# Where experts with few tokens are computed: 64-token steps of their own, or f32 pieces between the layers of a 256-token block

## The chip, the cores and the metric

The kernel runs on one core of one Trainium2 chip. The metric is the device time of one execution in microseconds (us), the median over three runs. Engines are called by their names or by the profile's short forms: TensorE (PE, its weight loads PEld), VectorE (DVE), ScalarE (ACT), GpSimd (POOL), and SyncE (SP), which here only issues DMAs. A q behind a short form (PEldq) means the engine's queue: branches, waits, loads of registers.

## The reference, cut to what matters

Three stages follow one another. Attention with a window gives `x` with 2304 tokens of 512 values. A mixture of 8 experts with one expert per token follows, then a dense block of two layers.

```python
e_idx = np.argmax(logits, axis=1)            # logits = x @ w_gate + modality_bias[modality_id]
...
for e in range(E):                           # E = 8
    mask = e_idx == e
    if not mask.any():
        continue
    h = np.maximum(x[mask] @ w1[e], 0.0)     # w1[e] 512 x 1024
    out[mask] = gate_w[mask, None] * (h @ w2[e])   # w2[e] 1024 x 512
...
h = x @ w_in                                 # 512 x 2048, then a quadratic relu
return (g @ w_out).astype(np.float32)        # 2048 x 512
```

How many tokens an expert gets depends on the data. With the inputs that `setup_inputs` draws (seed 0), the reference sends 19, 1735, 3, 0, 540, 6, 0 and 1 tokens to experts 0 to 7.

## The kernel before, in words

Everything large is computed in fp32r with the operands split into a hi and a lo half: three matmuls (hi x hi, lo x hi, hi x lo) stand for one f32 product. An expert's weights are 8 tiles of 128 x 1024 values (512 KB each, `raw`), four of `w1` and four of `w2`. `Weights.split` makes `whi` (a cast on ScalarE) and `wlo` (a subtraction on VectorE or GpSimd) of each.

The expert stage is a list of steps laid out at build time, up to 17, of which the counts decide at run time which do what. Small tables of the counts are computed on VectorE (`Route.late_counts`, `Route.registers`), written to the tile `ri` and loaded into registers of the engines (`Moe.values`, line 506). The expert with the most tokens among the first 512 goes first (here expert 1), and two half blocks of it are gathered while attention still runs. After that, experts come in cyclic order. Each expert's tokens fill blocks of 256 columns. A last block of at most 64 tokens runs in a narrow form, and a remainder of at most 64 beyond a full block makes that block 320 wide. With these inputs the steps are: 1 to 6 for expert 1, 7 narrow for expert 2, 8 and 9 (320 wide) for expert 4, 10 to 12 narrow for experts 5, 7 and 0. Steps 13 to 16 are skipped.

`Moe.step(s)` writes a step's work out in a fixed order: `layer1`, then gathers of later tokens on GpSimd and the first four weight splits for the next step (`resplit`), then loads of weights on SP, then `layer2`, the scaling of the gathered tokens on VectorE, the other four splits and loads. Every engine runs its own part in that order. `layer1` and `layer2` have three arms each (narrow, 256, 320), chosen by a register (lines 729, 747, 754, 767); every engine jumps over the arms that it doesn't take.

- `l1_wide(fb)`, eight times: 12 matmuls of 256 columns (line 587), a relu on ScalarE, the lo half of `h` on VectorE. Four PSUM banks (`A`) take turns.
- `l2_wide(d)`, four times: 24 matmuls, one copy to `xy` on ScalarE. Two banks (`B`).
- the narrow arms swap the operands: 64 tokens with hi and lo are the stationary operand (128 columns), the weights move (512 columns, lines 612 and 613). A matmul with `fold` (lines 619 and 764) adds the halves and transposes back.
- `tx`: eight transposes that bring the next step's tokens into `xh` and `xl`.

Between these runs `Convert`: it turns `w_in` and `w_out` (int64 words) into f32, in 32 parts of six VectorE operations (lines 813 to 825; the first can be ScalarE's), and stores them to DRAM (`wsc`). `CV_STEPS` says how many parts each step does in its first and second half: 20 in steps 2 to 5 and 12 in steps 6 to 8. Its loads and stores stand in SP's queue among the loads of expert weights. `Blocks` reads `wsc` back and splits it for the dense part, which goes over six groups of 384 tokens and writes each token to its place by an indirect DMA. `Route.positions` computes these places.

Of the kernel before, what the change touches and what calls it, by code (L numbers as in the profile page):

```python
# [23 lines left out]
HP = H // 2  # L24
# [26 lines left out]
YW = N + 192  # L51
# [3 lines left out]
LOADS = (0, 2, 1, 3, 4, 6, 5, 7)  # L55
R_M, R_CN, R_NE, R_C, R_D, R_O, R_N = range(7)
# [40 lines left out]
def body(ctx, tc, qT, kT, vW, mod, w_gate, m_bias, w1, w2, w_in, w_out, cst, msk, out):  # L97
# [9 lines left out]
    oh = keep.tile([128, NT + 1, E], BF16, name="oh")  # L107
# [4 lines left out]
    tri16 = const.tile([128, 128], BF16, name="tri16")  # L112
    one16 = const.tile([128, 128], BF16, name="one16")

    m2 = None
    with ExitStack() as st:
        banks = Banks(tc, st)
# [12 lines left out]
        cv.loads()  # L130
        late = ExitStack()
        for s in range(2, NS):
            moe.step(s, cv, m2, late=late)
            if s == CV_LAST:
                cv.close()
                m2 = Blocks(tc, ctx, wsc)
                m2.first()
        late.close()
    dense(tc, xy, m2, pid, out)


# [63 lines left out]
class Route:  # L205
    def __init__(self, tc, cs, oh, tri16, one16, banks, moe, pid):
# [25 lines left out]
        self.sm = p.tile([1, 8, 18], F32, name="rt_sm")  # L232
        self.sa = p.tile([1, 17, E], F32, name="rt_sa")
# [50 lines left out]
    def pick(self):  # L284
# [12 lines left out]
        V.tensor_scalar(self.sm[:, 0, 0:1], self.r8[0:1], -1.0, 8.0, op0=ALU.mult, op1=ALU.add)  # L297
        V.tensor_copy(self.moe.ri[:, R_M, 0:1], self.sm[:, 0, 0:1])
# [13 lines left out]
    def early_counts(self):  # L312
# [26 lines left out]
        V.tensor_scalar(self.pr[:, :, E], self.nAm, -1.0, None, op0=ALU.mult)  # L339

# [17 lines left out]
    def late_counts(self):  # L358
# [8 lines left out]
        V.tensor_scalar(self.k8, self.nM, 0.0, 256.0, op0=ALU.is_gt, op1=ALU.mult)  # L367
# [9 lines left out]
        hi, HI = self.tmp[:, :, E], self.HI  # L377
        V.tensor_tensor(HI, self.look[:, 0, :], hi, op=ALU.add)
        V.tensor_tensor(self.look[:, 1, :], hi, self.look[:, 1, :], op=ALU.is_ge)
        V.tensor_scalar(self.look[:, 0, :], HI, -0.5, 3968.0, op0=ALU.mult, op1=ALU.add)  # L380
        V.tensor_tensor(self.look[:, 0, :], self.look[:, 0, :], self.look[:, 1, :], op=ALU.mult)
        V.tensor_tensor(HI, HI, self.look[:, 0, :], op=ALU.add)
# [7 lines left out]
    def lookup(self, table, dst):  # L390
# [3 lines left out]
        nc.vector.tensor_reduce(dst, self.tmp, axis=AX.X, op=ALU.add)  # L394
# [4 lines left out]

    def rest_columns(self):  # L400
        self.columns(0, NT, self.HI, 16, 32)
# [5 lines left out]
    def registers(self):  # L407
        nc, cs, ri = self.tc.nc, self.cs, self.moe.ri
        P0 = slice(0, 1)
        b3, b4 = [1, 16, E], [1, 17, E]  # L410
        ta = cs[P0, C_TAU:C_TAU + 32:2]
        et, ex, cf, off, rem, u, mk, db = (self.sm[:, i, 0:17] for i in range(8))
        a, a4 = self.sa[:, 0:16], self.sa
        b8 = [128, E, E]
        V = nc.vector
        nb, ts, kk, q1 = self.nM[P0], self.tab[P0, 0, :], self.t8[P0], self.k8[P0]
        nAm, key = self.nAm[P0], self.key[P0]
        V.tensor_tensor(ts, ts, nAm, op=ALU.add)
        V.scalar_tensor_tensor(kk, nb, 0.0, key, op0=ALU.is_gt, op1=ALU.mult)
        V.tensor_tensor(a, ts.unsqueeze(1).to_broadcast(b3), ta.unsqueeze(2).to_broadcast(b3), op=ALU.is_le)  # L420
        V.tensor_tensor(a, a, kk.unsqueeze(1).to_broadcast(b3), op=ALU.mult)
        V.memset(et[:, 0:1], 0.0)
        V.tensor_reduce(et[:, 1:17], a, axis=AX.X, op=ALU.max)
        V.memset(cf[:, 0:1], 1.0)
        V.tensor_tensor(cf[:, 1:17], et[:, 1:17], et[:, 0:16], op=ALU.not_equal)
        V.tensor_copy(ri[:, R_C, 0:17], cf)
        V.tensor_tensor(a, key.unsqueeze(1).to_broadcast(b3), et[:, 1:17].unsqueeze(2).to_broadcast(b3), op=ALU.is_equal)
        V.tensor_tensor(q1, nb, ts, op=ALU.add)
        V.tensor_tensor(self.v[P0, 0:16], a, q1.unsqueeze(1).to_broadcast(b3), op=ALU.mult)
        V.tensor_reduce(rem[:, 1:17], self.v[P0, 0:16], axis=AX.X, op=ALU.add)  # L430
        V.tensor_tensor(rem[:, 1:17], rem[:, 1:17], ta, op=ALU.subtract)
        V.tensor_scalar(u[:, 1:17], rem[:, 1:17], 256.0, None, op0=ALU.is_gt)
        V.scalar_tensor_tensor(u[:, 1:17], rem[:, 1:17], 320.0, u[:, 1:17], op0=ALU.is_le, op1=ALU.mult)
        V.scalar_tensor_tensor(ri[:, R_D, 1:17], rem[:, 1:17], 64.0, u[:, 1:17], op0=ALU.is_gt, op1=ALU.add)
# [12 lines left out]
        V.tensor_tensor(self.pr[:, :, 0:E], self.nS.unsqueeze(1).to_broadcast(b8), self.tri, op=ALU.mult)
        V.tensor_reduce(self.s1, self.pr[:, :, 0:E], axis=AX.X, op=ALU.add)
        V.tensor_reduce(db[:, 0:1], self.n1[P0], axis=AX.X, op=ALU.add)
        V.tensor_scalar(ri[:, R_N, 0:1], db[:, 0:1], 1.0 / 256, None, op0=ALU.mult)  # L450
        V.tensor_scalar(u[:, 1:17], ta, db[:, 0:1], float(N), op0=ALU.is_ge, op1=ALU.mult)
        V.tensor_tensor(q1, self.s1[P0], nAm, op=ALU.add)
        V.tensor_tensor(q1, q1, ts, op=ALU.subtract)
        V.tensor_tensor(a, key.unsqueeze(1).to_broadcast(b3), et[:, 1:17].unsqueeze(2).to_broadcast(b3), op=ALU.is_equal)
        V.tensor_tensor(a, a, q1.unsqueeze(1).to_broadcast(b3), op=ALU.mult)
        V.tensor_reduce(off[:, 1:17], a, axis=AX.X, op=ALU.add)
        V.tensor_tensor(off[:, 1:17], off[:, 1:17], ta, op=ALU.add)
        V.tensor_tensor(off[:, 1:17], off[:, 1:17], u[:, 1:17], op=ALU.max)
# [17 lines left out]
class Moe:  # L476
    def __init__(self, tc, st, cs, xy, x_dram, w, banks):
# [4 lines left out]
        self.x = one.tile([128, HP, 5, 2, 64], F32R, name="x")  # L482
        self.xh, self.xl = self.x[:, :, :, 0, :], self.x[:, :, :, 1, :]
        self.h, self.hh, self.hl = [], [], []
        self.hidden(one)
        self.ids = one.tile([128, 2 * NS + 16], U32, name="ids")
        self.ri = one.tile([1, 7, NS], I32, name="ri")
# [3 lines left out]
    def hidden(self, pool):  # L491
        t = pool.tile([128, 4, 5, 2, 64], F32R, name=f"h{len(self.h)}")
        self.h.append(t)
        self.hh.append(t[:, :, :, 0, :])
        self.hl.append(t[:, :, :, 1, :])

    def rest(self, st):
        one = st.enter_context(self.tc.tile_pool(name="m_two", bufs=1))
        self.hidden(one)
        self.hs = one.tile([128, 2, 512], F32, name="hs")  # L500
        self.xg3 = one.tile([64, XW], F32, name="xg3")
        self.tc.nc.gpsimd.memset(self.xg3, 0.0)
# [6 lines left out]
    def expert(self, v):  # L509
        return self.tc.nc.s_assert_within(v, 0, E - 1, skip_runtime_bounds_check_because=BOUNDED)  # L510

    def load_first(self):
        return self.expert(self.values(R_M, R_M, 0, 1, [ENG.SP])[0])

    def load_sp(self, a, b):
        v = self.values(R_CN, R_NE, a, b, [ENG.SP])
        for i in range(b - a):
            r = self.regs.setdefault(a + i, {})
            r["cn"], r["ne"] = v[i], self.expert(v[b - a + i])

    def load_mode(self, a, b):
        c = self.values(R_C, R_C, a, b, [ENG.Activation, ENG.DVE, ENG.Pool])
        d = self.values(R_D, R_D, a, b, [ENG.PE, ENG.Activation, ENG.DVE, ENG.Pool])
        dp = self.values(R_D, R_D, a, b, [ENG.Pool])
        dv = self.values(R_D, R_D, a, b, [ENG.DVE])
# [130 lines left out]
    def load_w(self, s, a, b):  # L656
        if s >= NS:
            return
# [639 lines left out]
```

## Time and profile before

| | |
|---|---|
| median of 3 runs | 875.83 us (875.2 to 876.02) |
| profiled execution | 875.21 us, span 873.4 us |
| mean granted TensorE clock | 0.965 |
| PE busy | 796.6 us (91%) |
| PEld busy | 727.0 us (83%) |
| DVE busy | 523.3 us (60%) |
| ACT busy | 302.5 us (35%) |
| POOL busy | 150.5 us (17%) |
| loads of expert weights | 48 of 512 KB |

Times are counted from the span's start. Attention takes the time until about 130 us, the expert steps that until 454 us, dense the rest. [...] An engine's idle time is put down to what ended it; "issue" means that nothing in the profile was waited for. A plain f32 matmul leaves two records in the trace, an fp32r matmul or a transpose one.

### The profile page before, as it was taken

What the parts mean: (1) busy time and instruction counts of PE and PEld (TensorE: products, weight loads), DVE (VectorE), ACT (ScalarE), POOL (GpSimd) and SP (SyncE); (2) the same over time, 40 slices, a digit from 0 to 9 for tenths busy, and PEclk for the clock granted to TensorE, in tenths of its full rate; (3) what the DMA queues carried; (4) which work ended last, traced back from release to release, by engine and by line L of the source; (5) the groups of instructions that cost most, each with busy time, mean ns of one, the idle gap of its engine ahead of it and who ended that gap; (6) DMA issues with size and microseconds to landing.
All of it is one profiled execution on the core that took longest, in us unless ns stands there. A gap on an engine that the chain in (4) does not pass through costs nothing. (4 is left out here: it accounts for less than half of the span.)

```text
span 873.4 us, 15586 instructions
## 1 busy us (share of the span) xinstructions
PE 796.6 (91%) x5735; PEld 727.0 (83%) x5737; DVE 523.3 (60%) x1110; ACT 302.5 (35%) x775; POOL 150.5 (17%) x118
## 2 busy tenths in 40 slices
PE   8999698999998966699568999999999999999996
PEld 4887598999998956698467999999999999999995
DVE  4798967557767899547945764434434434444441
ACT  3665552222222343234333443223223223223221
POOL 2335632000000343025620001000000000000001
PEclk9999999999999988899697999999999999999999
DMA  7788633635656588526612420000000000000000
GB/s 188 225 249 266 200 104 87 226 131 189 207 155 223 195 277 285 164 76 198 207 32 76 144 73 25 13 1 24 13 1 25 13 2 13 24 1 13 25 2 36
DMA packets 54243, 96.23 MB, mean 110 GB/s; under 512 B 7104, under 2 KB 24512, under 8 KB 54112
## 3 DMA queue, kind: packets, MB, share of 16 engines
q1 hardware_dynamic: 49920, 80.71, 28.9%
q0 software_dynamic: 4048, 13.51, 5.2%
q8 instruction: 78, 1.28, 0.6%
q14 instruction: 53, 0.43, 0.2%
q10 hardware_dynamic: 144, 0.29, 0.1%
HBM read 76.53 MB, written 17.97 MB: 108 GB/s over the span
## 5 line engine op out<-in xcount | busy, mean ns | idle before, releaser
L1191 PE MATMUL psh<-yh,dwh 128*128 128x384 f32 x384 | 130.4, 340 | 8.8 <-DVE yh L1177 8.8
L1199 DVE SCALAR_TENSOR_TENSOR t<-t 128x384 f32<-128x384 f32 x96 | 53.5, 557 | 137.3 <-ACT t L1198 137.3
L1191 PE MATMUL psh<-yl,dwh 128*128 128x384 f32 x384 | 130.3, 339 | 0.0
L1191 PE MATMUL psh<-yh,dwl 128*128 128x384 f32 x384 | 129.9, 338 | 0.0
L1209 PE MATMUL pso<-dwh,gl 128*128 128x512 f32 x288 | 113.7, 395 | 0.0
L1209 PE MATMUL pso<-dwl,gh 128*128 128x512 f32 x288 | 113.6, 394 | 0.0
L587 PE MATMUL ps_e<-h,whi 128*128 128x256 f32 (+1 forms) x576 | 108.2, 286 | 4.5 <-ACT x L580 2.1
L1209 PE MATMUL pso<-dwh,gh 128*128 128x512 f32 x288 | 112.3, 390 | 0.0
L587 PEld LDWEIGHTS ps_e<-h,whi 128*128 128x128 f32 x576 | 90.3, 189 | 5.7 <-ACT x L580 2.5
L1201 ACT CAST gh<-t 128x384 fp32r<-128x384 f32 x96 | 49.4, 514 | 130.9 <-PE pso L1209 80.8
L1202 DVE TENSOR_TENSOR gl<-t,gh 128x384 fp32r<-128x384 f32 x96 | 53.6, 558 | 62.3 <-ACT gh L1201 62.3
L1198 ACT ACTIVATE t<-psh 128x384 f32<-128x384 f32 x96 | 47.1, 491 | 125.3 <-PE psh L1191 125.3
L1216 POOL DMA_INDIRECT out<-o,pid x18 | 17.5, 973 | 401.0 <-ACT o L1214 388.4
L1191 PEld LDWEIGHTS psh<-yh,dwh 128*128 128x128 f32 x384 | 73.0, 190 | 12.9 <-DVE yh L1177 8.9
L587 PE MATMUL ps_e<-h,wlo 128*128 128x256 f32 (+1 forms) x288 | 81.7, 284 | 0.0
L587 PE MATMUL ps_s<-x,whi 128*128 128x256 f32 (+1 forms) x304 | 65.5, 305 | 15.3 <-issue 8.5
L202 POOL TENSOR_TENSOR wlo<-raw,whi 128x1024 fp32r<-128x1024 f32 x23 | 66.8, 2906 | 65.6 <-ACT whi L200 32.1
L1191 PEld LDWEIGHTS psh<-yh,dwl 128*128 128x128 f32 x384 | 73.0, 190 | 3.6
L1191 PEld LDWEIGHTS psh<-yl,dwh 128*128 128x128 f32 x384 | 72.8, 189 | 0.0
L587 PEld LDWEIGHTS ps_s<-x,whi 128*128 128x128 f32 x304 | 53.1, 206 | 16.7 <-issue 9.4
L1209 PEld LDWEIGHTS pso<-dwh,gl 128*128 128x128 f32 x288 | 54.0, 188 | 11.8
L1209 PEld LDWEIGHTS pso<-dwl,gh 128*128 128x128 f32 x288 | 54.0, 188 | 9.3
(237 smaller groups left out, 1485.9 us busy)
## 6 DMA issues: line engine op xcount, KB each, us to landing
raw<-in_w SPq DMA_DIRECT2D x48, 512.0 KB, 5.8
r<-in_w_in SPq DMA_DIRECT2D x16, 512.0 KB, 6.0
r<-in_w_out SPq DMA_DIRECT2D x16, 512.0 KB, 6.5
wsc<-cva SPq DMA_DIRECT2D x32, 256.0 KB, 3.0
m2raw<-wsc SPq DMA_DIRECT2D x16, 512.0 KB, 3.5
v<-in_vW SPq DMA_DIRECT2D x16, 432.0 KB, 4.1
k<-in_kT SPq DMA_DIRECT2D x16, 304.0 KB, 5.0
q<-in_qT SPq DMA_DIRECT2D x16, 288.0 KB, 4.5
```

The lines of the kernel that those rows point to most:

```text
L202: eng.tensor_tensor(self.lo[i], t, self.hi[i].bitcast(F32), op=ALU.subtract)
L587: self.tc.nc.tensor.matmul(ps, a, b, start=(i == 0 and j == 0), stop=(i == n - 1 and j == 2))
L1191: nc.tensor.matmul(ps, a[k][:, 0, q], b[c], start=(c == 0 and j == 0), stop=(c == HP - 1 and j == 2))
L1198: nc.scalar.activation(t, ps, ACTF.Relu, scale=0.5, bias=0.5)
L1199: nc.vector.scalar_tensor_tensor(t, t, 1.0, t, op0=ALU.min, op1=ALU.mult)
L1201: nc.scalar.copy(gh, t)
L1202: nc.vector.tensor_tensor(gl, t, gh.bitcast(F32), op=ALU.subtract)
L1209: nc.tensor.matmul(po[g][i], a[:, q], b[k][:, 1, :], start=(k == 0 and j == 0), stop=(k == NFB - 1 and j == 2))
L1216: nc.gpsimd.indirect_dma_start(out=out[:, :], out_offset=bass.IndirectOffsetOnAxis(ap=pid[:, n:n + 1], axis=0), in_=o, in_offset=None)
```

## The change

An expert whose tokens don't fill a block no longer gets one, except the first expert: the counts are rounded to 256, and what is left of an expert, at most 64 tokens, is called small. A small block has no step of its own. It runs in five pieces inside a step with 256 tokens of another expert (or of its own, for a remainder), in plain f32 on the raw weights, without a split:

- `small_x` ahead of block 0 of the first layer: four transposes of 64 tokens, copied to `x32`
- `small_1` ahead of block 2: eight matmuls, 64 tokens stationary, 512 weight columns moving; even and odd slices go to the two halves of the output partitions
- `small_h` ahead of block 4: eight matmuls with `fold` add the halves and transpose, a relu
- `small_2` ahead of the second layer: eight matmuls as in `small_1`
- `small_y` ahead of its third block: four matmuls with `fold`, a copy to a gap behind `xy`, from where `close_gap` moves it in dense

Each piece stands under an `If` of its own on a register. The narrow arms and the 320-wide arms are gone. A small expert is put at a step after which the weights don't change (here experts 2, 5, 7 and 0 at steps 2 to 5), a remainder at its own expert's first step (step 7). Its raw weights are loaded during the step ahead of it. The transposes `tx` for the next step move behind `small_2`, to the head of the second half; all lo halves of weights move from GpSimd to VectorE; the conversion is spread over steps 2 to 7 with more parts in the second halves; the first splits of dense come in step 8; the steps are 15 at most, and steps 9 to 15 stand under nested `If`s as steps 9 to 16 did. The tables in `registers` are larger, and part of them comes before the second load of the token numbers.

```diff
-REGS_AT = {1: (1, 9), 4: (9, 17)}
-CV_STEPS = {2: (2, 3), 3: (2, 3), 4: (2, 3), 5: (2, 3), 6: (2, 2), 7: (2, 2), 8: (2, 2)}
+REGS_AT = {1: (1, 9), 7: (9, 16)}
+CV_STEPS = {2: (2, 3), 3: (2, 4), 4: (2, 4), 5: (2, 4), 6: (2, 3), 7: (0, 4)}
-NS = 17
+NS = 16
...
-        V.tensor_scalar(self.k8, self.nM, 0.0, 256.0, op0=ALU.is_gt, op1=ALU.mult)
+        V.scalar_tensor_tensor(self.k8, self.nM, 0.0, self.isM, op0=ALU.is_gt, op1=ALU.mult)
+        V.tensor_scalar(self.k8, self.k8, 256.0, None, op0=ALU.mult)
         V.scalar_tensor_tensor(n1, n1, R256, self.k8, op0=ALU.subtract, op1=ALU.max)
...
+    def small(self, s, piece):
+        if s < 1:
+            return
+        with self.tc.If(self.regs[s]["sm"] == 1):
+            piece(s)
+
+    def small_1(self, s):
+        nc, raw = self.tc.nc, self.w.keep
+        for h in range(2):
+            for c in range(HP):
+                j = c % 2
+                nc.tensor.matmul(self.b.B[h][64 * j:64 * j + 64, :], self.x32[:, c, :], raw[2 * h + c // 2][:, j, :],
+                                 start=(c < 2), stop=(c >= 2))
+            nc.scalar.copy(self.hs[:, h, :], self.b.B[h])
+
+    def small_h(self, s):
+        nc = self.tc.nc
+        ps = self.b.X[1].rearrange("p (f t) -> p f t", f=8)
+        for f in range(8):
+            nc.tensor.matmul(ps[:, f, :], self.hs[:, f // 4, (f % 4) * 128:(f % 4 + 1) * 128], self.fold, start=True, stop=True)
+        nc.scalar.activation(self.h32, ps, ACTF.Relu)
+
+    def small_2(self, s):
+        nc, raw = self.tc.nc, self.w.keep
+        for f in range(8):
+            j = f % 2
+            nc.tensor.matmul(self.b.A[0][64 * j:64 * j + 64, :], self.h32[:, f, :], raw[4 + f // 2][:, j, :],
+                             start=(f < 2), stop=(f >= 6))
+        nc.scalar.copy(self.hs[:, 0, :], self.b.A[0])
...
+    def half_a(self, s, wide, parts, cv):
...
+        pieces = {0: self.small_x, 2: self.small_1, 4: self.small_h}
+        for fb in range(8):
+            if fb in pieces:
+                self.small(s, pieces[fb])
+            if wide:
+                self.l1_wide(fb)
+                next(c_work, None)
+                next(c_work, None)
...
+    def half_b(self, s, wide):
+        self.small(s, self.small_2)
+        if wide:
+            self.tx(s + 1, 0)
+            self.tx(s + 1, 1)
+        off = bass.ds(self.regs[s]["off"], 256)
+        for d in range(HP):
+            if d == 2:
+                self.small(s, self.small_y)
+            if wide:
+                self.l2_wide(d, off)
...
     def step(self, s, cv=None, rt=None, late=None):
...
+        self.either(s, lambda wide: self.half_a(s, wide, cv.start(n[0]) if n[0] else [], cv))
+        self.load_w(s, 0, 4)
         self.gather3(s + 1)
         self.resplit(s + 1, 0, 4)
+        if s == CV_LAST + 1:
+            self.m2.first()
...
+        self.either(s, lambda wide: self.half_b(s, wide))
+        self.gather(s + 3)
+        self.load_w(s, 4, 8)
         if cv:
-            for p in cv.start(CV_STEPS[s][1]):
+            for p in cv.start(n[1]):
                 for _ in cv.ops(*p, act=False):
                     pass
+        self.scale3(s + 1)
+        self.scale(s + 2)
         self.resplit(s + 1, 4, 8)
...
                 for i in range(a, b):
-                    self.w.split(i, i in (1, 3, 5), i in (1, 3, 5))
+                    self.w.split(i, False)
...
             if k == 0:
+                if g == 3:
+                    close_gap()
                 ysplit(g)
```

`gather3` and `scale3` fetch and scale the tokens of a small block (before: the 64 extra ones of a 320-wide block). `either` runs a half as it stands, and at steps 7 and 8 under a test of the number of blocks in use, with the pieces alone as the other arm.

## Rows read from the trace of the kernel before

**Rows 1.** Busy time by stage: window, its us, busy us per engine, granted clock, DMA.

```profile
180.50:204.30 23.80, 23.80 (x201) 23.80 (x201) 17.69 (x39) 6.31 (x15) 1.90 (x2) 1.00 0.60 202
204.30:306.90 102.60, 96.83 (x803) 95.55 (x802) 77.15 (x155) 28.91 (x66) 13.38 (x10) 1.00 0.59 191
306.90:333.50 26.60, 13.41 (x83) 11.93 (x81) 26.08 (x35) 13.31 (x21) 12.84 (x5) 0.83 0.87 288
333.50:363.70 30.20, 26.64 (x201) 26.06 (x202) 25.52 (x48) 6.84 (x16) 7.43 (x4) 0.92 0.67 206
363.70:399.60 35.90, 31.00 (x205) 30.86 (x205) 17.20 (x20) 9.86 (x17) 7.64 (x4) 0.90 0.41 127
399.60:453.90 54.30, 39.16 (x242) 34.21 (x240) 43.06 (x38) 25.53 (x44) 28.45 (x13) 0.87 0.47 150
453.90:462.60 8.70, 0.00 (x0) 0.01 (x1) 0.51 (x2) 0.82 (x3) 0.00 (x0) 0.72 0.05 10
462.60:873.40 410.80, 403.83 (x2016) 365.89 (x2016) 186.56 (x326) 125.88 (x246) 17.52 (x18) 0.99 0.08 28
```

**Rows 2.** Timeline of TensorE: start, us, operation, idle before it and its releaser.

```profile
333.46 0.57 PE L587 MATMUL ps_s<-x,whi 128*128 128x256 f32 x1 [5.83 <-issue]
...
430.39 0.55 PE L612 MATMUL ps_e<-whi,h 128*128 128x256 f32 x1 [3.55 <-DVE whi L198]
```

**Rows 3.** TensorE's branches at two lines: ns min/median/max, first and last start.

```profile
L754 PEldq COMPARE_BRANCH  x16: 75/219/5996, 166.1 to 453.2; - x16
...
L138 PEldq COMPARE_BRANCH  x6: 67/72/4793, 359.9 to 461.9; - x6
```

**Rows 4.** Timeline of TensorE: f32 matmuls of attention, and folds of step 11.

```profile
124.97 0.69 PE L1026 MATMUL ps_o<-pt,v 96*64 96x64 f32 x16
125.58 0.39 PE L587 MATMUL ps_s<-x,whi 128*128 128x256 f32 x1
...
424.12 1.00 PE L619 MATMUL ps_e<-cs,hs 128*128 128x64 f32 x8
```

**Rows 5.** Single lines: ns min/median/max of one, first and last start.

```profile
L1026 PE MATMUL ps_o<-pt,v x576: 222/222/369, 20.5 to 125.4; 96*64 96x64 f32 x192
...
L577 PE MATMUL ps_r<-cs,xga x24: 270/272/280, 166.9 to 425.3; 128*128 128x128 f32 x24
...
L580 ACT CAST x<-ps_r x13: 578/586/587, 146.7 to 445.5; 128x512 fp32r<-128x512 f32 x13
...
L506 DVEq TENSOR_LOAD <-ri x6: 605/1844/2446, 148.9 to 245.5; - x6
...
L202 DVE TENSOR_TENSOR wlo<-raw,whi x25: 1207/1219/3431, 295.3 to 444.4; 128x1024 fp32r<-128x1024 f32 x25
```

**Rows 6.** Timeline of VectorE from 145 to 155 us (register tables).

```profile
145.69 0.49 DVE L570 TENSOR_SCALAR xgb<-xgb 128x512 f32<-128x512 f32 x1 [0.90 <-DMA xgb<-x_dram,ids]
...
146.96 0.28 DVE L436 TENSOR_TENSOR rt_sa<-rt_key,rt_sm 1x136 f32<-1x136 f32 x1
...
148.90 0.17 DVE L445 TENSOR_TENSOR ri<-rt_sm 1x17 int32<-1x17 f32 x1
...
154.06 0.23 DVE L447 TENSOR_TENSOR rt_pr<-rt_nS,rt_tri 128x64 f32<-128x64 f32 x1 [3.81 <-DVEq L704]
```

**Rows 7.** Timelines of TensorE and VectorE, second half of step 3.

```profile
215.83 0.60 PE L577 MATMUL ps_r<-cs,xga 128*128 128x128 f32 x4
...
219.06 0.43 DVE L815 TENSOR_SCALAR cva<-r 128x512 int32<-128x512 int32 x1 [0.69 <-DVEq L704]
...
221.99 0.42 DVE L815 TENSOR_SCALAR cva<-r 128x512 int32<-128x512 int32 x1
```

**Rows 8.** DMA issues of the page: count, KB each, median us to landing.

```profile
raw<-in_w SPq DMA_DIRECT2D x48, 512.0 KB, 5.8
r<-in_w_in SPq DMA_DIRECT2D x16, 512.0 KB, 6.0
...
wsc<-cva SPq DMA_DIRECT2D x32, 256.0 KB, 3.0
```

More of the change, by code (lines that the diff above doesn't have):

```diff
@@ L132, in body @@
         for s in range(2, NS):
-            moe.step(s, cv, m2, late=late)
+            moe.step(s, cv, late=late)
             if s == CV_LAST:
                 cv.close()
-                m2 = Blocks(tc, ctx, wsc)
-                m2.first()
+                m2 = moe.m2 = Blocks(tc, ctx, wsc)
         late.close()
-    dense(tc, xy, m2, pid, out)
+    dense(tc, xy, m2, pid, out, moe.close_gap)
 class Banks:
@@ L408, in registers @@
         nc, cs, ri = self.tc.nc, self.cs, self.moe.ri
+        V = nc.vector
         P0 = slice(0, 1)
[L410 to L422, printed above, removed]
+        b16, b8 = [128, 16, E], [128, E, E]
+        ta = cs[:, C_TAU:C_TAU + 32:2]
+        it = cs[:, C_E:C_E + E]
+        et, cf, nt, N_, u, mk, db, el = (self.sm[:, i, 0:17] for i in range(8))
@@ new lines, in registers @@
+        a, mt, pr = self.sa[:, 0:16], self.mt, self.pr[:, :, 0:E]
+        n1, key, ts, kk = self.n1, self.key, self.tab[:, 0, :], self.t8
+        r, small, idx, lt, S = (self.ex[:, i, :] for i in range(5))
+        V.tensor_tensor(ts, ts, self.nAm, op=ALU.add)
+        V.scalar_tensor_tensor(kk, n1, 0.0, key, op0=ALU.is_gt, op1=ALU.mult)
+        V.tensor_tensor(a, ts.unsqueeze(1).to_broadcast(b16), ta.unsqueeze(2).to_broadcast(b16), op=ALU.is_le)
+        V.tensor_tensor(a, a, kk.unsqueeze(1).to_broadcast(b16), op=ALU.mult)
@@ L515, in load_sp, with load_regs @@
+    def load_regs(self, name, row, a, b, engines):
+        for i, v in enumerate(self.values(row, row, a, b, engines)):
+            self.regs.setdefault(a + i, {})[name] = v
     def load_sp(self, a, b):
-        v = self.values(R_CN, R_NE, a, b, [ENG.SP])
+        v = self.values(R_LD, R_NE, a, b, [ENG.SP])
         for i in range(b - a):
             r = self.regs.setdefault(a + i, {})
-            r["cn"], r["ne"] = v[i], self.expert(v[b - a + i])
+            r["ld"], r["ne"] = v[i], self.within(v[b - a + i], 0, E - 1)
@@ new lines, in small_y, with close_gap @@
+    def small_y(self, s):
+        nc = self.tc.nc
+        ps = self.b.A[1][:, 0:256].rearrange("p (c t) -> p c t", c=HP)
+        for c in range(HP):
+            nc.tensor.matmul(ps[:, c, :], self.hs[:, 0, c * 128:(c + 1) * 128], self.fold, start=True, stop=True)
+        nc.scalar.copy(self.xy[:, :, bass.ds(self.regs[s]["so"], 64)], ps)
+    def close_gap(self):
+        tc, nc, xy = self.tc, self.tc.nc, self.xy
+        n, t = self.gap
+        with ExitStack() as st:
+            for i in range(8):
+                st.enter_context(tc.If(n >= 64 * i + 1))
+                a = self.within(t + 64 * i, 0, N)
+                b = self.within(t + (64 * i + GAP), 0, N + GAP)
+                nc.gpsimd.tensor_copy(xy[:, :, bass.ds(a, 64)], xy[:, :, bass.ds(b, 64)])
@@ L1156, in attention, with dense @@
             emit_store()
-def dense(tc, xy, m2, pid, out):
+def dense(tc, xy, m2, pid, out, close_gap):
     nc = tc.nc
```

367 lines of the change are left out of this document (173 added, 194 removed).

## Prediction, made before the changed kernel was run

> **What bounds the kernel now.** I read the busy shares by stage first, then the order of time inside the expert stage, then single lines. By stage [rows 1], the dense part from 462.6 us is 410.8 us of nearly unbroken TensorE (PE 403.8 busy). The change hardly touches it. The expert stage is where time is: a 256-token step takes 23.8 us where nothing disturbs it (201 matmuls and transposes, PE busy throughout), and four such steps with no change of weights take 102.6, 7.4 more than undisturbed. The rest is dearer. The first 64-token step takes 26.6 us with PE busy for 13.4, the 256-token step after it 30.2, the 320-token step 35.9, the last three 64-token steps together 54.3, and 8.7 more pass with PE idle until dense begins. So PE sets the end wherever it is fed, and from 306.9 to 462.6 us it is not.
>
> What ends its idle time is seen at two places [rows 2]: 5.83 us before the matmul at 333.46 with "issue" as releaser, and 3.55 us at 430.39 until VectorE had made a weight half. The 5.83 us belong to a branch: TensorE's queue shows branches of up to 6.0 us, where half of them take 0.22 or less [rows 3]. The jump over the two wide arms is such a one.
>
> [...]
>
> **What will run.** The reference's own inputs give 19, 1735, 3, 0, 540, 6, 0 and 1 tokens per expert. 256 of expert 1 are done ahead of step 1. Before, 12 further steps follow: six for expert 1, a 64-token one for expert 2, 256 + 284 tokens of expert 4, and 64-token ones for experts 5, 7 and 0. That is the order in rows 1. After, `n1` keeps six blocks for expert 1 and two for expert 4 (steps 7 and 8). Experts 2, 5, 7 and 0 ride in steps 2 to 5, expert 4's last 28 tokens in step 7.
>
> **What goes.** From rows 1, with 23.8 us for a clean step:
> - first 64-token step: 26.6; the other three: 54.3.
> - the 320-token step becomes a 256-token one: 35.9 - 23.8 = 12.1.
> - the disturbed step at 333.5: 30.2 - 23.8 = 6.4 (the new change of weights is charged below).
> - steps 3 to 6: 102.6 - 4 x 23.8 = 7.4. Between their halves TensorE jumped over the unused arms; these arms are gone. Bounds 0 and 7.4; I take all, since step 2 shows none of it.
> - the gap before dense: PE leaves the last 64-token step by one long branch and the unused steps by another, of 4.8 us [rows 3]; afterwards only the second is left. With about 0.2 us at its end to the first halves of y and their 0.6 us, 5.6 or less remain; I take 5.0, since PE's queue runs a little ahead of its matmuls. So 3.7 go, bounds 0 and 6.
> Together 110.5 us.
>
> **What a small block costs on PE.** No row has an f32 matmul with a 512-column moving operand. The nearest are the f32 matmuls of attention, whose outputs also alternate between two halves of the partitions: 16 records (two per matmul) take 0.69 us from 124.97 on and the next operation starts at 125.58 [rows 4]. Less the last one's 0.22 that is (0.69 - 0.22)/15 = 31 ns per record of 64 columns, so 0.25 us for 512 columns. Singly, a record grows from 222 ns at 64 columns to 272 at 128 [rows 5], 0.8 ns per column, so 0.41 us for 512. I take 0.25, because the two halves alternate in the same way here, and keep 0.41 as the other end. `small_1` and `small_2` have 16 records each: 32 x 0.25 = 8.0 us. The folds have 16 + 8 records of the kind that ran 8 in 1.00 us [rows 4], about 0.1 each without the last one's tail: 2.4. Four transposes take 0.4 (0.60 us for the group at 215.83 [rows 7], less the last one's tail). Changing from 64 to 128 output columns costs 0.15 us: the last of the 16 records starts at 124.97 + 15 x 0.031 = 125.43, the next matmul at 125.58. Four times: 0.6. Sum 11.4, five times: 57.0 us. With 0.41 it is 16.5 and 82.5.
>
> [...]
>
> A piece's evacuation by ScalarE (0.59 us for 512 columns [rows 5]) lies beside the two blocks of `l1_wide` between pieces (24 of the clean step's 201 operations, 2.8 us). If that cover went, PE would wait about 0.6 us at each of four pieces.
>
> **What else is added.**
> - Register tables, ahead of step 1. VectorE's small operations stand 0.2 us apart (ten from 146.96 to 148.90 [rows 6]). The parts ahead of the mode registers grow from 10 to about 38 operations, but the first part shrinks and `scale(1)` waits for its gather until 145.69 anyway [rows 6]. From 146.1 20 operations, the columns (0.9) and 18 operations end at about 154.4, against 149.05. VectorE then loads two sets of registers instead of three (1.84 us in the median [rows 5]). The join after them, at which VectorE went on at 154.06 [rows 6] and on which TensorE waited too, comes at 157.4: +3.4. The later part (28 operations, 5.5 us) ends before the first PSUM bank is needed again. Bounds 0 and 9.
> - VectorE's own queue. In steps 3 to 5 it converts four parts behind `small_2` and the transposes. A part takes 2.93 us (219.06 to 221.99 [rows 7]). From the start of a second half: 4.05 (`small_2`) + 3.2 (transposes to the first conversion, 215.83 to 219.06) + 11.7 + 0.8 for `scale3` = 19.8 us, while PE is through after 4.05 + 0.9 + 11.4 + 0.95 = 17.3. The next `small_x` stands first in PE's queue and waits: 2.5 us, twice (3 to 4, 4 to 5; step 6 has no small block). +5.0, bounds 0 and 10.
> - Change of weights, 6 to 7. Eight lo halves go to VectorE at 1.22 us [rows 5], none to GpSimd. Four of them, the transposes' lo, three parts (8.8) and `scale3` end 16.9 us after the first half; PE's second half takes 12.3. [...] +7.0, bounds 2 and 12.
> - Skipped pieces. Steps 1, 6 and 8 jump over five each. A skipped `If` also waits for its engine's own semaphore, so PE cannot run ahead: about 0.4 us (a matmul's latency and a short branch), 15 times: +6.0. Bounds 0 and 10.
> - The weights of the small experts are as many bytes as before, moved to steps 1 to 4. `load_w` for step s+1 is issued about one step ahead, behind the conversion's stores on SP. `close_gap` is one GpSimd copy with GpSimd idle. Zero for both; price below.
>
> Sum added: 57.0 + 3.4 + 5.0 + 7.0 + 6.0 = 78.4. Net 78.4 - 110.5 = -32.1. The profiled execution took 875.21 us (span 873.4 and 1.8 around it), 0.6 under the median of 875.83, so **843 us**.
>
> **Rivals.**
> - A, the halves don't overlap: 16.5 per block, +25.5, while the 5.0 of VectorE's wait goes: 864. For it: K is 96 rows there and 128 here, and 512 columns were never seen. Against it: 31 ns is under half of what 0.8 ns per column gives.
> - B, slower than before: the small experts' weights land late. Place: `small_1` in steps 2 to 5, PE's queue standing on the load. One step moves 8 x 512 KB of weights, 6 x 512 KB in, 6 x 256 KB out [rows 8] and 0.5 MB of gathers: 9.5 MB. At the 288 GB/s of the first 64-token step (DMA share 0.87) this takes 33 us and fits the step's 35.2. At 191 to 202 GB/s, as in the clean steps, it takes 47 to 50: +12 to +15, four times, 891 to 903. It decides at 220 GB/s, +8.0 per step. Against it: those clean steps had a share of only 0.6.
> [...]
> - D, the change doesn't do what it says, because fewer blocks fall away: only if the counts were others; the six sets of 8 weight loads [rows 8] and the step lengths agree with them.
>
> **Chances and range.** Forecast 0.73, A 0.13, B 0.07, C 0.05, D 0.02. With the least of each bound (57 + 2 added) the time is 875.2 - 110.5 + 59 = 824; mild cases of both sides, A and most of C are inside 820 to 867. What this kernel's measurement can tell from no change is 0.2%. Faster by more than that: forecast, A, C and a share of the rest, 0.92; within it 0.02; slower 0.06 (B).
>
> **What would show it.** Right: nine steps instead of thirteen, dense beginning at about 429 us, a block's PE operations at 11 to 12 us, pairs of f32 records at half the spacing of single ones, PE waiting for VectorE's `scale3` at steps 4, 5 and 7. Wrong: `small_1` with 0.4 us per record (A), PE idle until a DMA of `raw` (B), long branches at the skipped pieces (C), or steps 2 to 5 longer than 40 us for a reason not named here.

## The result and the profile after

| | before | after |
|---|---|---|
| median | 875.9 us (4 runs, 875.2 to 878.1) | 843.2 us (4 runs, 839.7 to 845.2) |
| profiled execution | 875.21 us, span 873.4 | 841.64 us, span 839.6 |
| mean granted clock (share of full speed) | 0.965 | 0.979 |
| PE busy | 796.6 us (91%) | 793.6 us (95%) |
| DVE busy | 523.3 us (60%) | 461.8 us (55%) |
| POOL busy | 150.5 us (17%) | 98.7 us (12%) |

The changed kernel takes 0.962 of the time before, 95% interval 0.958 to 0.966. Forecast were 843 us and a range of 820 to 867. The 875.83 us given above are the median of the first three runs of the kernel before; with the fourth it is 875.9. TensorE is busy for nearly as long as before; what went is its idle time.

First the same view by stage as [rows 1], of the changed kernel: window, its length, busy us of PE, PEld, DVE, ACT and POOL with counts, granted clock (1.00 is full speed), DMA share, GB/s. The lines are step 1, steps 2 to 8, the gap ahead of dense, and dense.

```profile
154.00:188.00 34.00, 29.09 (x236) 27.91 (x235) 18.25 (x57) 5.39 (x14) 4.92 (x5) 0.86 0.48 161
188.00:222.60 34.60, 34.60 (x264) 29.08 (x261) 19.25 (x42) 9.52 (x22) 2.83 (x3) 1.00 0.79 271
222.60:258.70 36.10, 34.63 (x262) 29.05 (x261) 21.07 (x46) 10.19 (x23) 2.83 (x3) 1.00 0.74 245
258.70:294.80 36.10, 34.64 (x260) 29.05 (x260) 21.88 (x48) 9.85 (x22) 2.83 (x3) 1.00 0.79 267
294.80:331.10 36.30, 36.14 (x261) 30.47 (x261) 20.65 (x45) 9.61 (x22) 1.91 (x2) 0.95 0.45 147
331.10:362.00 30.90, 24.88 (x200) 23.95 (x200) 24.19 (x48) 14.23 (x25) 2.93 (x3) 0.99 0.91 303
362.00:400.70 38.70, 37.35 (x260) 31.49 (x261) 20.62 (x39) 9.09 (x21) 1.91 (x2) 0.92 0.27 83
400.70:426.40 25.70, 24.90 (x200) 24.03 (x200) 9.43 (x18) 7.42 (x16) 2.53 (x2) 1.00 0.37 117
426.40:429.80 3.40, 0.00 (x1) 0.01 (x1) 0.38 (x2) 0.66 (x2) 0.00 (x0) 0.97 0.03 7
429.80:839.60 409.80, 403.15 (x2016) 365.18 (x2016) 186.87 (x326) 126.01 (x247) 17.98 (x19) 0.99 0.08 28
```

Step 2 shows a small block with nothing else in the way: 34.6 us with PE busy throughout, 10.8 over the clean step's 23.8. Steps 3 and 4 are 1.5 longer, step 5 is 1.7 longer at a lower clock (0.95), the step with a change of weights ahead (331.1) and the one after it (362.0) clearly more.

Next TensorE's timeline after, with the idle time before an operation in brackets: the block's f32 work in step 2, then the places where PE stood longest.

```profile
155.45 0.66 PE L271 MATMUL ps_e<-rt_hv,rt_LO 128*128 128x16 f16 x18 [6.41 <-DVE xl L622]
167.10 0.58 PE L628 MATMUL ps_s<-xh,whi 128*128 128x256 f32 x1 [2.61 <-DVE hl L639]
...
191.47 3.65 PE L667 MATMUL ps_e<-raw,x 128*64 128x512 f32 x16
198.03 1.89 PE L675 MATMUL ps_s<-cs,hs 128*128 128x64 f32 x16
205.66 3.65 PE L682 MATMUL ps_s<-raw,h 128*64 128x512 f32 x16
215.89 1.00 PE L690 MATMUL ps_s<-cs,hs 128*128 128x64 f32 x8
...
258.69 0.46 PE L659 MATMUL ps_r<-cs,xg 64*128 64x64 f32 x4 [1.47 <-DVE xg L603]
294.81 0.46 PE L659 MATMUL ps_r<-cs,xg 64*128 64x64 f32 x4 [1.47 <-DVE xg L603]
351.88 0.39 PE L628 MATMUL ps_e<-hh,whi 128*128 128x256 f32 x1 [1.26 <-ACT xy L647]
362.05 0.69 PE L659 MATMUL ps_r<-cs,xg 64*128 64x64 f32 x4 [4.21 <-DVE xg L603]
368.71 3.65 PE L667 MATMUL ps_e<-raw,x 128*64 128x512 f32 x16 [0.56 <-ACT x L660]
429.80 0.69 PE L1244 MATMUL psh<-yh,dwh 128*128 128x384 f32 x1 [3.42 <-DVE yh L1230]
```

L659 to L690 are `small_x`, `small_1`, `small_h`, `small_2` and `small_y`; L603 is `scale3`, L628 the wide matmul. The three waits for `scale3` stand where the prediction put them, ahead of steps 4, 5 and 7, and the 8.70 us between the last step and dense [rows 1] have become 3.40.

### The profile page after: what moved, and what is told of

It reads as the page before. It is cut to its first block, busy times and chain, and to the rows that moved or that the text cites. A ratio compares the mean times of both kernels' runs of the same rounds, so it can differ in the third digit from the quotient of the medians.

```text
span 839.6 us, 15178 instructions
## 1 busy us (share of the span) xinstructions
PE 793.6 (95%) x5713; PEld 701.6 (84%) x5713; DVE 461.8 (55%) x1100; ACT 281.5 (34%) x744; POOL 98.7 (12%) x100
## 5 line engine op out<-in xcount | busy, mean ns | idle before, releaser
L1255 DVE TENSOR_TENSOR gl<-t,gh 128x384 fp32r<-128x384 f32 x96 | 53.8, 561 | 62.5 <-ACT gh L1254 61.9
L628 PE MATMUL ps_e<-hh,whi 128*128 128x256 f32 x288 | 82.7, 287 | 1.6 <-ACT xy L647 1.3
L628 PE MATMUL ps_e<-hl,whi 128*128 128x256 f32 x288 | 81.3, 282 | 0.0
L628 PE MATMUL ps_e<-hh,wlo 128*128 128x256 f32 x288 | 81.1, 281 | 0.0
L1262 PEld LDWEIGHTS pso<-dwh,gh 128*128 128x128 f32 x288 | 54.1, 188 | 8.9
L1047 ACT ACTIVATE p<-ps_s,nb 128x96 f32<-128x96 f32 x144 | 47.1, 346 | 34.1 <-DVE su L1055 33.3
L628 PEld LDWEIGHTS ps_e<-hh,whi 128*128 128x128 f32 x288 | 54.6, 190 | 2.1 <-ACT xy L647 1.5
```

Source lines behind the costliest of these rows:

```text
L628: self.tc.nc.tensor.matmul(ps, a, b, start=(i == 0 and j == 0), stop=(i == n - 1 and j == 2))
L1047: nc.scalar.activation(p[:, j, :], s[:, j, :], ACTF.Exp, scale=scale, bias=nb[:, j:j + 1], accum_out=su[:, j:j + 1])
L1255: nc.vector.tensor_tensor(gl, t, gh.bitcast(F32), op=ALU.subtract)
L1262: nc.tensor.matmul(po[g][i], a[:, q], b[k][:, 1, :], start=(k == 0 and j == 0), stop=(k == NFB - 1 and j == 2))
```

## The experiments

All start from the changed kernel, 843.2 us; each ratio is to the kernel before, measured beside it on the same chip (there 875.4 to 876.4 us).

**one_half: rival A, the halves don't overlap.**

```diff
-                nc.tensor.matmul(self.b.B[h][64 * j:64 * j + 64, :], self.x32[:, c, :], raw[2 * h + c // 2][:, j, :],
-                                 start=(c < 2), stop=(c >= 2))
+                nc.tensor.matmul(self.b.B[h][0:64, :], self.x32[:, c, :], raw[2 * h + c // 2][:, j, :],
+                                 start=(c == 0), stop=(c == HP - 1))
...
-            nc.tensor.matmul(self.b.A[0][64 * j:64 * j + 64, :], self.h32[:, f, :], raw[4 + f // 2][:, j, :],
-                             start=(f < 2), stop=(f >= 6))
+            nc.tensor.matmul(self.b.A[0][0:64, :], self.h32[:, f, :], raw[4 + f // 2][:, j, :],
+                             start=(f == 0), stop=(f == 7))
```

> The f32 matmuls of small_1 and small_2 all write the lower 64 partitions of one bank instead of alternating between its two halves; the folds then read 64 rows. Theory (the halves run at the same time): in the changed kernel 16 records take 3.65 us, 0.20 us apart with a tail of 0.59; without the pairing they stand 0.41 apart, so 32 x 0.21 = 6.7 us more per block, 33 in five blocks, less 3 to 5 because PE then no longer waits for VectorE's scale3 at steps 4 and 5: 871 to 876 us. Rival (0.20 us is what one record takes by itself and the halves do nothing): 843 us, records still 0.20 apart.

Measured: 878.6 us, ratio 1.0036 (1.0017 to 1.0055): slightly slower than before. The block's first matmuls on TensorE's timeline:

```profile
191.98 7.08 PE L667 MATMUL ps_e<-raw,x 128*64 128x512 f32 x16
```

3.65 us became 7.08: (7.08 - 0.59)/15 = 0.43 us per record where (3.65 - 0.59)/15 = 0.20 stood (a record lasts 0.59 in both). The 0.20 is a mean. In the changed kernel two records start 0.006 us apart and the next two 0.42 us later; in one_half each starts 0.43 us after the last. A window of 0.24 us between two starts, for L667 alone, holds two records in the changed kernel (first line) and one in one_half (second):

```profile
192.12:192.36 0.24, 0.24 (x2) 1.00 1.05 384
192.63:192.88 0.25, 0.25 (x1) 1.00 1.14 463
```

So a record is no shorter for being paired; the two halves run side by side. Twice 3.43 in five blocks is 34.3 of the 35.4 us. The theory holds; its 3 to 5 us off were wrong, since PE still waited 1.1 us for `scale3` at steps 4 and 5. With unpaired halves the whole change would have gained nothing.

**no_skips and no_small: the price of the Ifs, and of all five blocks.**

```diff
# no_skips
-        with self.tc.If(self.regs[s]["sm"] == 1):
+        if s in (2, 3, 4, 5, 7):
             piece(s)
# no_small
-        V.tensor_copy(ri[:, R_SM, 0:17], db[P0])
-        V.memset(ri[:, R_SM, 0:1], 0)
+        V.memset(ri[:, R_SM, 0:17], 0)
```

In no_small the row of loads is cleared of the small experts too, so the kernel leaves their tokens out.

> The five pieces are put into steps 2, 3, 4, 5 and 7 alone, without an If, so steps 1, 6 and 8 have no piece to jump over (with these inputs nothing is left out). Theory: a skipped piece costs PE 0.31 us between l1 blocks and 0.46 at small_2, 1.7 per step, 5.1 for three steps: 838 us, steps 8 and 6 1.7 us shorter. [...] Rival 2 (the pauses stand beside waits that end later anyway): 843.

> No small block runs and none of the small experts' weights is loaded (the 57 tokens of experts 2, 5, 7, 0 and of expert 4's remainder are left out). Theory: five blocks of 10.8 us go (54.0), 25 more skipped pieces come (+8.5), the waits for scale3 at steps 4, 5 and 7 and the lower clock after them go (4 to 12): 843 - 54 + 8.5 - 4 to 12 = 786 to 794 us. Rival 1 (the weights' transfers or VectorE's queue also slow the wide layers): under 780. Rival 2 (the blocks fill time in which PE would stand anyway): over 805.

Measured: no_skips 837.8 us (0.9554, 0.9533 to 0.9575), 5.4 less. That is near the theory's 5.1, but the trace doesn't show the gain where the theory put it. Two waits of TensorE in no_skips, in step 6 and ahead of dense:

```profile
337.98 0.39 PE L628 MATMUL ps_s<-xh,whi 128*128 128x256 f32 x1 [1.92 <-DVE hl L639]
427.31 0.66 PE L1242 MATMUL psh<-yh,dwh 128*128 128x384 f32 x1 [5.24 <-DVE yl L1229]
```

The matmuls of step 8 do end 1.7 us sooner after the step's start (23.95 us for 25.65), but the wait ahead of dense is 5.24 us for 3.42. Step 6 takes 31.8 us for 31.0, since the new wait of 1.92 us and a granted clock of 0.72 behind it replace the pauses. The profiled executions differ by 2.4 us (839.25 and 841.64), and 1.8 of them lie in step 5, where the wait of 1.47 us was here followed by a clock of 1.00. So the pauses are shown as time of TensorE; that taking them out gives the 5.1 us is not shown. Steps 6 and 8 of this execution look as rival 2 has it; why dense waits longer is open.

In the changed kernel TensorE's branches at the pieces' `If` take 63 to 337 ns (min, median, max; first and last start):

```profile
L652 PEldq COMPARE_BRANCH  x65: 63/169/337, 155.6 to 418.0; - x65
```

no_small 792.4 us (0.9035, 0.9018 to 0.9053): the blocks together cost 50.8 us net, inside the theory's 49 to 57. Neither rival holds.

**twice_loaded: rival B, the transfers are at their limit.**

```diff
         nc.sync.dma_start(t, src)
+        x = self.scr.tile([128, 2, 512], F32, name=...)   # a tile in DRAM
+        nc.sync.dma_start(x, src)
```

> Behind each load of a weight tile from step 0 on, the same 512 KB are copied once more to a spare area in memory: 4.2 MB more per set of weights, read and written. Theory (in steps 2 to 5 the weights land 21 us before small_1 and small_2 read them: 204.2 for 226.0 and 219.5 for 240.2; only the set for step 7, landing at 345 to 361 us, is used at once): steps 2 to 4 as long as before, at step 7 up to 10 us more, 843 to 856 us. Rival (B of the prediction, the transfers are at their limit): 4.2 MB at 264 GB/s are 16 us, in four or five steps, 907 to 923 us.

Measured: 853.8 us (0.9756, 0.9736 to 0.9775), 10.5 more, inside the theory. Steps 2, 3 and 4 of this kernel by window:

```profile
188.60:223.15 34.55, 34.55 (x262) 29.04 (x260) 19.22 (x42) 9.36 (x22) 2.82 (x3) 1.00 1.04 373
223.15:259.26 36.11, 34.66 (x262) 29.06 (x261) 21.04 (x46) 10.20 (x23) 2.82 (x3) 1.00 1.04 376
259.26:295.36 36.10, 34.64 (x260) 29.05 (x260) 21.75 (x48) 9.52 (x22) 2.83 (x3) 1.00 1.04 379
```

They move 373 to 379 GB/s instead of 245 to 271 in the same 34.6, 36.1 and 36.1 us. The loads do land later (the set for step 3 at 209.6 and 225.2 us instead of 204.2 and 219.5), but still 15 to 17 us before their use. The extra time lies at the change of weights. PE waits 9.43 us there for ScalarE's `xy` copy, which stands behind the weight casts, the last of them waiting for a tile that lands at 356.54 us (349.23 in the changed kernel). PE's row, then ScalarE's:

```profile
359.13 0.58 PE L633 MATMUL ps_e<-hh,whi 128*128 128x256 f32 x1 [9.43 <-ACT xy L652]
356.57 1.04 ACT L206 CAST whi<-raw 128x1024 fp32r<-128x1024 f32 x1 [2.70 <-DMA raw<-in_w]
```

So steps 2 to 4 have room for later loads, and the change of weights has none.

**scale_first, then scale_first_regs7: VectorE's queue, and what comes after it.**

```diff
# both
+        self.scale3(s + 1)
         if cv:
             for p in cv.start(n[1]):
...
-        self.scale3(s + 1)
# scale_first_regs7 in addition: step 7's load_sp, load_mode and load_off go from ahead of half_a to behind it
```

> scale3 of the next step stands ahead of the conversion's parts in VectorE's queue instead of behind them. Theory (PE's idle time before small_x at steps 4, 5 and 7 is VectorE's queue, and the lower clock after two of these is their consequence): 1.47 + 1.47 + 4.21 us of idle time and about 1.2 + 3.3 us of lower clock go, 11.6 in all: 831 to 833 us. Rival 1 (the wait only moves: VectorE is as late as before, and PE stands at the fifth l1 block for its hl): 843. Rival 2 (the clock falls whatever PE's idle time is): 836, with a granted clock near 0.5 still to be seen early in steps 5 and 7.

Measured: 841.8 us (0.9615, 0.9592 to 0.9638), 1.4 less, which the intervals don't tell from the changed kernel: the theory missed by ten. Rival 2 fell too: the granted clock is 1.00 in the first 6 us of steps 5 and 7. Rival 1's 843 is met, but for another reason than it gave. TensorE's longest waits from 150 to 430 us (line, released by, us in total, times, longest):

```profile
PE ps_e L667 <- ACT x L660: 7.5, 1, 7.5
PE ps_e L271 <- DVE xl L622: 6.4, 1, 6.4
PE ps_s L628 <- DVE hl L639: 4.1, 2, 2.4
PE psh L1244 <- DVE yh L1230: 3.5, 1, 3.5
```

The waits for `scale3` are gone, steps 2 to 5 get 4.5 us shorter and step 6 gets 3.4 shorter. But step 7 is 5.9 longer: 7.5 us appear one place later, before `small_1` of step 7, until ScalarE has copied `x32`, and the granted clock is 0.72 in the 6 us after them. ScalarE stood in step 7's four register loads:

```profile
L549 ACTq TENSOR_LOAD <-ri x4: 1370/1537/1567, 359.2 to 363.8; - x4
```

In the changed kernel the same four loads lie from 361.9 to 368.0, nearly hidden by the 4.21 us wait and the low clock that follows it; PE saw 0.56 of them.

> scale_first once more, and step 7's register loads for steps 9 to 15 (four on ScalarE, 6.2 us, which stood ahead of its copy of x32) moved behind step 7's first half. Theory (in scale_first the wait before small_x(7) turned into 7.5 us before small_1(7) because ScalarE stood in these loads): small_1(7) follows small_x(7) after 3.5 to 4 us, no granted clock under 1.0 in step 7, 7 us less than scale_first: 834 to 835 us. Rival (what holds step 7 is the landing of its weights, at 361 us, and the split's lo halves): the wait moves to the first l2 block of step 7, 839 to 842 us.

Measured: 835.9 us (0.9536, 0.9519 to 0.9553), 5.9 less than scale_first against 7 expected. No wait for `scale3` is left, but 2.18 us before `small_1(7)`. ScalarE's timeline shows their cause:

```profile
357.96 1.05 ACT L201 CAST whi<-raw 128x1024 fp32r<-128x1024 f32 x1 [0.27 <-DMA raw<-in_w]
359.55 1.04 ACT L201 CAST whi<-raw 128x1024 fp32r<-128x1024 f32 x1 [0.55 <-DVE xga L610]
360.51 0.37 ACT L660 COPY x<-ps_r 128x256 f32<-128x256 f32 x1
```

The copy now stands directly behind the last two weight casts. The first waited 0.27 us for its load; the wait of 0.55 before the second is put down to VectorE's scaling of `xga`, its load having landed 0.4 us before it started (at 359.1). So of the rival, the weights' landing, a small part at most is left, and at another place than it said: the casts ahead of the copy are the next limit.

**late_regs, then regs_second: the tables ahead of step 1.**

```diff
# both: the six operations of ri[R_SM] directly behind lt, ahead of the columns and of ri[R_NE]
# late_regs
-                next(regs)            # fourth part, at d == 0
+                next(regs)            # at d == 2, behind tx(1)
...
-        next(regs, None)              # last part and load_off: ahead of half_a(1)
+        # last part and load_off: behind half_a(1)
# regs_second
+                self.load_regs("c", R_C, 1, 9, [ENG.Activation, ENG.DVE])   # behind the first part
...
-        self.load_mode(1, 9)
         self.resplit(1, 0, 8)
+        self.load_small(1, 9)         # the other registers
...
+            if s == 1 and fb == 4:    # last part inside half_a; load_off behind it
+                next(self.last_regs, None)
```

> VectorE computes the row of the small blocks' steps ahead of the columns and the experts' row, tx(1) stands ahead of the fourth part of the tables, and the last part (28 operations) and ScalarE's register loads for the offsets move behind the first half of step 1. Theory (PE's 6.4 us before the third placement are VectorE's chain plus PE's own register load, its 2.6 us in half_a(1) the loads on ScalarE's queue): the row is ready 2.8 us earlier and the 2.6 us go, step 2 begins at 182.5 to 183.5 instead of 188.0, 837.5 to 838.5 us from 843. Rival (the moved operations are late for what comes behind the first half: positions, tx(2), the second half's copies): PE stands at the next placement or at small_x(2), 843.

Measured: 848.4 us (0.9681, 0.9661 to 0.9702), 5 us slower; the theory fell. TensorE's timeline in step 1:

```profile
153.17 0.59 PE L271 MATMUL ps_e<-rt_hv,rt_LO 128*128 128x16 f16 x18 [2.75 <-DVE rt_hv L267]
159.47 0.58 PE L628 MATMUL ps_s<-xh,wlo 128*128 128x256 f32 x1 [5.20 <-DVEq L824]
...
185.82 0.58 PE L628 MATMUL ps_e<-hh,whi 128*128 128x256 f32 x1 [4.42 <-ACT xy L647]
```

The placement does come earlier, but two new waits cost more. Putting `tx(1)` ahead made the fourth part later, and with it the join of the weights' `If`, on which the first `wlo` matmul waits. The last part then ended so late that ScalarE's loads of the offsets held its `xy` copies.

> A second way of putting step 1's tables: the register loads that say whether weights change come behind the first part, in VectorE's wait for the gather; the join for the weights stands directly behind the fourth part, ahead of the other register loads; the last part (28 operations) stands inside half_a(1), between its fourth and fifth block; ScalarE's loads of the offsets stand behind half_a(1). Theory (late_regs failed because the join came 2.6 us later and because ScalarE's loads waited for a last part that had become late): the second l1 matmul starts about 155.7 instead of 156.9, no wait over 0.5 us at the fifth block and none over 1 us in half_b(1), step 2 begins at 183 to 184.5 instead of 188.0: 838.5 to 840 us from 843. Rival (the register loads themselves, 1.85 us a set, only change their place in the chain): 843 to 848.

Measured: 838.5 us (0.9573, 0.9551 to 0.9595), 4.7 less, as expected, though its interval still overlaps the changed kernel's (from 0.9578), and not at the times expected: this execution's attention ended 2.6 us later. The stretch that was changed says more. From the placement of the late ids to `small_x(2)` it takes 45.1 us, in the changed kernel 49.8, in late_regs 53.8.

**gpsimd_lo: undo the move of the lo halves.**

```diff
-                    self.w.split(i, False)
+                    self.w.split(i, i in (1, 3, 5))      # lo half on GpSimd
```

> At a change of weights three of the eight lo halves (1, 3 and 5) go to GpSimd again, as in the kernel before, the rest stays with VectorE. Theory (the 4.2 us before small_x(7) are VectorE's queue: two lo halves of 1.22 us less stand ahead of its conversion and scale3): the wait falls to 1.8 us and the lower clock after it is shorter: 3 to 5 us off 843, 838 to 840. Rival 1 (the lo halves stand in the queue until their weights land, the last of the first four at 349.2 us, so fewer of them end hardly earlier): under 1.5 us, 841.5 to 843. Rival 2 (GpSimd's 2.5 us each, twice VectorE's, hold the first l1 block of step 7 or the second half of step 6): slower than 843.

Measured: 846.2 us (0.9667, 0.9641 to 0.9694). The intervals overlap with the changed kernel's, so the times alone say only that it doesn't help. The traces say why: the wait before `small_x(7)` grew from 4.21 to 7.01 us. First GpSimd's, then VectorE's timeline of this kernel:

```profile
349.59 2.41 POOL L203 TENSOR_TENSOR wlo<-raw,whi 128x1024 fp32r<-128x1024 f32 x1 [14.34 <-DMA raw<-in_w]
352.23 3.10 POOL L203 TENSOR_TENSOR wlo<-raw,whi 128x1024 fp32r<-128x1024 f32 x1 [0.23 <-PEq L652]
362.03 2.71 POOL L203 TENSOR_TENSOR wlo<-raw,whi 128x1024 fp32r<-128x1024 f32 x1 [4.19 <-ACT whi L201]
```

```profile
350.87 2.21 DVE L203 TENSOR_TENSOR wlo<-raw,whi 128x1024 fp32r<-128x1024 f32 x1 [1.50 <-ACT whi L201]
354.20 1.41 DVE L867 TENSOR_SCALAR cva<-r 128x512 int32<-128x512 int32 x1
359.53 0.42 DVE L873 TENSOR_SCALAR cva<-cva 128x512 f32<-128x512 f32 x1
362.45 2.57 DVE L873 TENSOR_SCALAR cva<-cva 128x512 f32<-128x512 f32 x1
```

Each of GpSimd's three operations stretched one of VectorE's: 2.21 us for 1.22, 1.41 for 0.42, 2.57 for 0.42, ending within 0.3 us of GpSimd's end each time except for the first (1.1). And nothing was saved in the first four halves: VectorE is through with them 20.5 us after the step's start, 20.6 in the changed kernel, because it now waits 1.50 us for a cast. There rival 1 was right. The other two stretched operations (1.0 and 2.15 us) then make `scale3` 3.1 us later. The theory's 838 to 840 fell. Two VectorE operations with one input from PSUM (`xl`, at 353.00 and 353.60) took their usual 0.68 us beside GpSimd's second. Why some are stretched and others are not is open.

**all_three and best: do the gains add?** all_three is late_regs with scale_first_regs7, best is regs_second with it.

> late_regs and scale_first_regs7 together. Theory (the two stand at different places of the step order, so their gains add): 4.5 + 8.5 us off 843, 829 to 831 us. Rival (an earlier step 1 brings the change of weights 6 to 7 forward against transfers that don't come earlier): part of the gain of late_regs is lost at step 7, 832 to 835 us.

> regs_second and scale_first_regs7 together. Theory (different places, gains add, as the loss of late_regs and the gain of scale_first_regs7 did in all_three): 836 less 3.5 to 5: 831 to 832.5 us. Rival (the weights for step 7 don't land earlier, so what is gained at step 1 is waited for at step 7): 834 to 836.

Measured: all_three 840.8 us (0.9592, 0.9576 to 0.9609). Its expectation rested on a gain of late_regs; with the loss of 5.1 measured there and the gain of 7.3 one gets 841.0, so the two do add. best 831.0 us (0.9501, 0.9481 to 0.9521): 843.2 - 4.7 - 7.3 = 831.2. It beats both kernels, the changed one by 12 us. What its TensorE still waits longest for, from 150 to 420 us:

```profile
PE psh L1250 <- DVE yh L1236: 3.6, 1, 3.6
PE ps_e L271 <- DVE rt_hv L267: 2.8, 1, 2.8
PE ps_s L631 <- DVEq L828: 2.3, 1, 2.3
PE ps_e L670 <- ACT x L663: 2.2, 1, 2.2
PE ps_s L631 <- DVE hl L642: 1.6, 1, 1.6
```

## Why the prediction was right, term by term

Dense starts at 429.80 us, 32.8 earlier than in [rows 1], dense itself is 1.0 shorter, and 0.2 us more lie around the span: the profiled execution is 33.6 us shorter, forecast were 32.1. Of the 32.8, 1.3 belong to no term: attention, which the change leaves alone, was ahead by that much in this execution. The late ids are placed at 138.23 us, before at 139.54, and in the experiments between 138.2 and 140.8.

| term | predicted | measured | from |
|---|---|---|---|
| five small blocks | 57.0 | 54.0 | step 2: 34.6 - 23.8 = 10.8, five times |
| tables ahead of step 1 | 3.4 | 7.1 | 49.8 us from the placement of the late ids to step 2, 41.0 in the kernel before, less 1.7 for skipped pieces |
| VectorE at steps 4 and 5 | 5.0 | 4.3 | twice 1.47, and 1.4 at a lower clock in step 5 |
| change of weights 6 to 7 | 7.0 | 9.5 | 30.9 + 38.7 - 23.8 - 34.6 - 1.7 for skipped pieces |
| skipped pieces | 6.0 | 5.1 | three times 1.7 |
| sum added | 78.4 | 80.0 | |
| removed | 110.5 | 111.5 | 80.0 + 32.8 - 1.3 |

Every cause that the prediction named is there, and the two that carry it are shown: blocks fall away, and paired f32 matmuls make the small blocks cheap. That the total comes so close is in part luck. The added terms were off by -3.0, +3.7, -0.7, +2.5 and -0.9 us, 10.8 in all, of which 1.6 are left in the sum. The forecast's own sum also gives 843.7 (875.83 - 32.1), where it says 843.

- **The block, and rival A.** The value taken (0.25 us per record, from attention's paired records [rows 4]) was near the 0.20 measured, and the other end, 0.41 from the growth with columns [rows 5], is what an unpaired record takes: 0.43. The choice between them decided the sign: one_half. A change of shape cost about what was taken (in step 2, 0.09 us on the way into `small_1` and 0.20 behind it, for twice 0.15). The price the prediction gave for A, 25.5 us, was 10 too low, because 0.20 and 0.43 lie further apart than 0.25 and 0.41. It took off another 5.0 for VectorE's wait, which did not vanish.
- **Tables.** This is the term that was furthest off. VectorE went on behind the join at 156.94 us against 154.06 [rows 6], +2.9, or +4.2 counted from the placement of the late ids, where +3.4 was worked out. Most of the rest is a wait that the prediction hadn't seen: 2.61 us at the fifth block of step 1. ScalarE's next loads of two rows of offsets instead of one wait for the last part of the tables, and its first relu of the step runs only at 166.20. late_regs took this wait away with a later join, regs_second with an earlier one, so the two are separate.
- **VectorE's queue.** Each wait was 1.47 us where 2.5 was forecast. scale_first removes both by order alone, and steps 2 to 5 get 4.5 us shorter, so the cause is shown. The lower clock after one of the two was not forecast there.
- **Change of weights.** The term of 7.0 is a wait of 4.6 us (16.9 less 12.3) and 2.4 for a lower clock behind it, the author's estimate from the 0.92 over 30.2 us that follow the idle time of 5.83 [rows 1, 2]. No run shows these 2.4; in the changed kernel the wait is 4.21 us, and the clock of 0.50 in the 6.1 us after it costs about 3.0. 1.26 us more go to ScalarE's copy at 351.88. Left out was what lay just behind: ScalarE's register loads (6.2 us) and the landing of the weights, which scale_first and twice_loaded brought out.
- **Skipped pieces.** PE's spacing between blocks of step 8 grows from 0.12 to 0.43 us, and to 0.58 at `small_2`: 4 x 0.31 + 0.46 = 1.7 per step against 2.0 forecast. That is TensorE's time; in no_skips part of it turned up again as longer waits. The 0.4 us per piece were the author's estimate. The long branches at the pieces (C) did not come: none took more than 337 ns.
- **Rival B.** The bytes were as forecast (245 to 271 GB/s in steps 2 to 4 are 8.8 to 9.6 MB per step, 9.5 were worked out), but the loads are due much later than the rival assumed: the set for step 3 landed at 204.2 (first half) and 219.5 us (second), used at 226.0 and 240.2. The rates lie above its 220 GB/s, and the 373 to 379 of twice_loaded show what room was left.
- **What went.** Nine steps ran where 13 had, five of them with a small block, so rival D falls. The gap before dense fell to 3.4 us, not 5.0; the other removals come to 106.2 against 106.8 forecast. This tests little: the added terms are measured as what the steps have beyond the clean step's 23.8 us, so what remains has to be the rows of before. No run undid a removal singly, and their split rests on these rows.

## What to carry to other kernels

Before you price an f32 matmul with half the output columns, look at whether neighbours write different halves of the partitions: here that was 0.20 us per record against 0.43, and the whole gain. When you remove a wait, list everything queued behind the same point on every engine, register loads included: of two reorderings that took a wait away, one moved it to ScalarE and the other made two new ones. Read a long chain of small operations by its joins: in late_regs the first `wlo` matmul stood 5.20 us at the `If` of the weights until VectorE had passed it. And when a sum comes out, check its terms one by one: here errors of 10.8 us left 1.6.

## What the runs showed of the hardware

- **Clock after idle time.** In the profiles of the changed kernel and the eleven experiments, from step 1 to the start of dense, TensorE stood idle for 0.9 to 1.8 us 24 times; in the 6 us after it the granted clock was 1.00 in 19 and 0.72 in 5 of them. Of the 54 idle times of 1.9 us and more it was below 0.8 in 53. The same 1.47 us at step 5 were followed by 0.72 in the changed kernel and 1.00 in no_skips: what a short wait costs differed from one profiled execution to another. Why it did is open.
- **Two f32 records at once.** With 64 output columns each and 512 moving columns, records that write different halves of the partitions start two per 0.42 us in the changed kernel; in one_half, where all write one half, one starts per 0.43 us.
- **Register loads.** One `TENSOR_LOAD` of a row takes ScalarE 1.36 to 1.57 us in step 7 (changed kernel and scale_first), and 1.75 to 1.78 around the start of step 1 (changed kernel).
- **GpSimd and VectorE side by side.** In gpsimd_lo a VectorE operation that takes 0.42 us at 359.53 took 2.57 us beside a subtraction of 2.71 us on GpSimd.
